# Other places for seven products, PReLU halves issued by engine, and a scaling done a unit ahead

## The chip, the cores and the metric

The kernel runs on one core of a Trainium2 chip. What counts is the device time of one execution in microseconds (us), as the median of several runs. A profile is one such execution, recorded by the hardware profiler.

The engines are named as the profile names them: PE is TensorE (PEld its weight loads), DVE is VectorE, ACT is ScalarE, POOL is GpSimd, SP is SyncE, which issues most DMAs. Each engine works through its own instructions in the order in which they were written.

## The reference, cut to what matters

A state-space block (4 sequences of 768 positions, 8 heads of 32, state of 16) feeds a feed-forward layer with a PReLU (3072 tokens, 256 wide, 2048 hidden).

```
for c in range(nc):                      # chunks of the sequence
    L = exp(cum[i] - cum[j]) * causal    # decay inside the chunk
    y = ((C @ B.T) * L) @ x + (C @ state) * exp(cum)
    state = exp(sum(la)) * state + (B * decay_from_j).T @ x
h = y @ w_in
g = np.maximum(h, 0.0) + alpha * np.minimum(h, 0.0)
out = g @ w_out
```

## The kernel before

**Work.** The tokens are cut into 6 groups of 512. Group 0 goes through the feed-forward layer as it stands, while weights are loaded (the first 102.6 us). Groups 1 to 5 use a scheme with seven instead of eight block products for each of the two matrix products: sums of weights (`ws`) and of tokens (`xs`) are formed beforehand, and seven products are combined into the four output blocks.

**Units.** A group g has four units, z = 0 to 3, each for 512 of the 2048 hidden features. A unit is the function `quad`. Its seven first products (`first`, two matmuls each) go into two PSUM banks, A and Y. ACT and DVE form the four hidden blocks g12, g22, g21 and g11 from them, each by a call of `prelu`; g12, g21 and g11 are read from a bank, g22 from `c22` in SBUF. Between g12 and g22 ACT copies `m1` into Y (L645), since Y is used again. POOL then forms four differences of the blocks (`ta`, `tb`, `tc_`, `td`, L650 and L659). The seven products with `w_out` of a unit (`product`, L592) are run within the next unit, at places that the table `places` gives.

**PReLU.** For each half p of a block, ACT multiplies by alpha (L600) and DVE takes the maximum (L601). In a PSUM bank both engines read the same bank, and the framework makes each wait until the other has left it.

**Order.** All engines' orders are written out by hand: `quad` calls `after(1)` to `after(14)` between its steps, and `after(j)` runs what the tables put there. `places` maps j to one of the products 1 to 7. `steps` maps (z, j) to a stage of the state-space work for the next group, which comes as two pairs of chunks, each in nine stages: transposes of B and C with `cd` (0), two stages that write `cz` and each run one scan for the decays `dec` (1, 2; L375, DVE), the state update from `bn` (3; L445 on PE), two scans for the second chunk (4, 5), two stages of Gram matmuls into the two buffers `ss`, each followed by two DVE products with `dec` (6, 7; L476, L481), and the output y with its copy to `xT` (8). A scan stands on DVE in the same queue as the PReLUs. `bn`, B scaled by decays, is formed on POOL in stage 0 (`pair_loads`, L327).

**Combine.** The seven products of a finished group lie in four PSUM banks. `combine` (L677 to L692) adds them up during z=0 of the next group, in steps at j = 5, 9, 13 and 14; one sum, `u4`, is formed on POOL and read by DVE (L692). `finish` transposes the two results on DVE (L703) and writes them out, at (1, 4) and (1, 5).

**Loads.** `load_pair` issues a pair's loads on SP: `nat` (B and C), `xt`, `ap` and the broadcast decays `abc`, a pair or two ahead.

Of the kernel before, what the change touches and what calls it, by code (L numbers as in the profile page):

```python
# [22 lines left out]
def kernel(  # L23
# [25 lines left out]
    nc = tc.nc  # L49
# [304 lines left out]
    def pair(gp):  # L354
# [27 lines left out]
        if gp == 0:  # L382
            ahead[0] = spread(z, 0)
            rows_turn(0, rows_scan(0))
        elif gp == 6:
            rows_turn(1, held["pr"])
        bn = pair_loads(gp)

        pf = ap
        if not abc:  # L390
# [204 lines left out]

    def prelu(o, h, z, i):

        for p in range(2):
            f = 4 * z + 2 * p + i
            nc.scalar.mul(o[:, p], h[:, p], s_alpha[:, f : f + 1])  # L600
            nc.vector.scalar_tensor_tensor(out=o[:, p], in0=h[:, p], scalar=s_mul[:, f : f + 1],  # L601
                                           in1=o[:, p], op0=ALU.mult, op1=ALU.max)

    def quad(g, z, after):


# [24 lines left out]
        first(A, lambda q: s2[:, q], t2)
        u2 = tile_of(wtp, "u2", "wg")
        nc.scalar.copy(out=u2, in_=A)  # L633
        after(4)
        after(5)
        nc.vector.tensor_tensor(out=Y, in0=Y, in1=u2, op=ALU.add)
        after(6)
        first(A, lambda q: wi[:, q, 1, 0], t3)
        c22 = tile_of(wtp, "c22", "wg")
        nc.vector.tensor_tensor(out=c22, in0=A, in1=m5, op=ALU.add)  # L640
        after(7)
        first(Y, lambda q: s4[:, q], b22)
        g12, g22, g21, g11 = (tile_of(gp, "gt", "gt") for i in range(4))
        prelu(g12, Y, z, 0)
        nc.scalar.copy(out=Y, in_=m1)  # L645
        prelu(g22, c22, z, 1)
        after(8)
        after(9)
        ta, tb, tc_, td = (tile_of(gp, "gt", "gt") for i in range(4))
        nc.gpsimd.tensor_tensor(out=tc_, in0=g22, in1=g12, op=ALU.subtract)  # L650
        after(10)
        first(A, lambda q: wi[:, q, 1, 1], t4)
        prelu(g21, A, z, 1)
        after(11)
# [12 lines left out]
    def combine(g):  # L667


        m = {n: ms[g][i][:, h] for n, (i, h) in HALVES.items()}  # L670
        sa = wtp.tile([P, 2, HT], F32, name="sa", tag="wr")
        u = wtp.tile([P, 2, HT], F32, name="u", tag="wr")
        u4 = op.tile([P, HT], F32, name="u4", tag="o_sb")
        c = [one.tile([P, 2, HT], F32, name=f"c{i}") for i in range(2)]
        last = g == NG - 1
        engs = [nc.sync, nc.scalar]
        nc.scalar.copy(out=sa[:, 0], in_=m[1])  # L677
        nc.vector.tensor_tensor(out=c[0][:, 0], in0=m[2], in1=sa[:, 0], op=ALU.add)
        if last:
            turn(g, 0, c[0], slice(0, HT), engs)  # L680
        yield
        nc.scalar.copy(out=sa[:, 1], in_=m[5])
        yield
        nc.vector.tensor_tensor(out=u[:, 0], in0=m[6], in1=sa[:, 0], op=ALU.add)
        nc.vector.tensor_tensor(out=u[:, 1], in0=m[7], in1=u[:, 0], op=ALU.add)
        nc.gpsimd.tensor_tensor(out=u4, in0=u[:, 0], in1=sa[:, 1], op=ALU.add)
        nc.gpsimd.tensor_tensor(out=c[1][:, 1], in0=u[:, 1], in1=sa[:, 1], op=ALU.add)
        yield
        nc.vector.tensor_tensor(out=c[1][:, 0], in0=u[:, 1], in1=m[4], op=ALU.subtract)
        if last:  # L690
            turn(g, 1, c[1], slice(0, GT), engs)
        nc.vector.tensor_tensor(out=c[0][:, 1], in0=m[3], in1=u4, op=ALU.add)  # L692
        ms.pop(g)
        if last:
            turn(g, 0, c[0], slice(HT, GT), engs)
        else:
            ends_of[g] = c

    def turn(g, i, c, ts, engs):
# [11 lines left out]
    def finish(g, i):  # L711
        turn(g, i, ends_of[g][i], slice(0, GT), [nc.sync])
# [28 lines left out]
    for n in range(2):  # L741
        for f in range(NF):
# [17 lines left out]
            if n and f in in_steps:  # L760
# [9 lines left out]

    places = {3: 1, 5: 2, 6: 3, 9: 5, 10: 7, 13: 6, 14: 4}
    for i in range(NZ * (NG - 1)):
        g, z = divmod(NZ + i, NZ)
        nxt = 2 * g + 2
# [1 line left out]
        def after(j, g=g, z=z, i=i, nxt=nxt):  # L776
            if i and j in places:
                product(*divmod(NZ + i - 1, NZ), places[j])
            if i == 0:
                if j in (3, 5, 6, 9):  # L780
                    output(NF - LAG + (j > 5), {3: 0, 5: 1, 6: 0, 9: 1}[j])
                if j == 2:
                    weight_sums(wi, in_sums, 4, 3)
                if j in (3, 5, 7):
                    weight_sums(wqt, out_sums, 0, {3: 0, 5: 1, 7: 2}[j])
                if j == 10:
                    weight_sums(wqt, out_sums, 0, 3)
            if i == 1 and j in (1, 4, 7, 9):
                weight_sums(wqt, out_sums, 4, {1: 0, 4: 1, 7: 2, 9: 3}[j])
            if g > 1 and z == 0 and j in (5, 9, 13, 14):  # L790
                if j == 5:
                    comb[0] = combine(g - 1)
                next(comb[0], None)
            if g > 1 and z == 1 and j in (4, 5):
                finish(g - 1, j - 4)
            if nxt < NP and (z, j) in steps:
                ssm(nxt + steps[z, j])
            if nxt < NP and (z, j) == (3, 6):
                token_sums(g + 1)
# [45 lines left out]
```

## Time and profile before

| | us |
|---|---|
| median of 3 runs | 471.69 (470.42 to 472.87) |
| the profiled execution's own time | 472.52 |
| its span, first to last instruction | 470.4 |
| mean granted PE clock, share of full speed | 0.954 |
| busy time of PE, DVE, POOL, ACT | 406.8, 269.5, 217.6, 183.8 |

A profile gives each engine's busy time and, for each idle stretch, the instruction whose end released the engine. The time of a run is a little longer than the span. Busy time on PE is modelled from overlapping matmuls; a row "x4" stands for the four records of two matmuls, and the start of the next row minus its own start is what they cost PE. PEclk is the clock that the chip granted to PE as a share of 2.4 GHz; 0.5 is 1.2 GHz.

### The profile page before, as it was taken

The page shows a single profiled execution, that of the slowest core. Times are in us where ns is not written, and L with a number is a line of the kernel's source. Part 1 is how long each engine was busy: PE and PEld are TensorE (multiplying, and loading weights), DVE is VectorE, ACT ScalarE, POOL GpSimd, SP SyncE. Part 2 cuts the span into 40 slices and gives each one's busy share as a digit, 9 for nine tenths or more (in the row PEclk, how much of TensorE's full clock was granted, in tenths as well). Part 3 has the DMA queues.
Part 4 walks back from the last instruction along what each step waited for, and adds up shares of the span by engine and source line. Part 5 has one row for each costly group of instructions (what it writes and reads, how often), then busy time and mean ns, then how long its engine had stood idle before and what let it go on. Part 6 is the DMA issues. An engine that isn't in the chain of part 4 may idle for free.

```text
span 470.4 us, 5917 instructions
## 1 busy us (share of the span) xinstructions
PE 406.8 (86%) x2131; PEld 302.9 (64%) x2131; DVE 269.5 (57%) x460; ACT 183.8 (39%) x408; POOL 217.6 (46%) x189
## 2 busy tenths in 40 slices
PE   6778899996998978599897869998859989989994
PEld 4446477785677667377585647766637767767773
DVE  5898966746457363548545555746363854353443
ACT  4556525235163263225433405326221543434430
POOL 2336745874835461607435232646260643453322
PEclk9999799999799998979998989999897999999998
DMA  9949961008506101055401017510102000002002
GB/s 215 258 157 247 220 138 49 1 8 191 100 2 111 36 1 45 0 81 125 86 0 46 1 23 125 100 46 0 46 0 45 1 1 1 0 5 42 0 0 46
DMA packets 124125, 30.58 MB, mean 65 GB/s; under 512 B 96880, under 2 KB 120000, under 8 KB 124096
## 3 DMA queue, kind: packets, MB, share of 16 engines
q1 hardware_dynamic: 117792, 29.67, 28.2%
q10 hardware_dynamic: 6304, 0.52, 0.9%
q8 instruction: 17, 0.28, 0.2%
q14 instruction: 12, 0.10, 0.1%
HBM read 26.85 MB, written 3.34 MB: 64 GB/s over the span
## 4 chain that ended last, share of the span: by engine, by line
PE 49%; DVE 22%; ACT 13%; POOL 10%; issue 4%; DMA 1%; POOLq 0%; ACTq 0%; DVEq 0%
PE hp L616 15%; PE bank L592 13%; DVE gt L601 12%; ACT gt L600 9%; POOL gt L659 7%; PE bank L535 5%; PE ss L476 4%; PE hp L522 4%; ACT hp L645 2%; DVE dec L375 2%; DVE dec L481 2%; PE ss L499 2%; DVE dec L370 1%; POOL xs L575 1%; PE ss L445 1%
## 5 line engine op out<-in xcount | busy, mean ns | idle before, releaser
L659 POOL TENSOR_TENSOR gt<-gt 128x512 f32<-128x512 f32 x58 | 91.2, 1572 | 36.1 <-DVE gt L601 25.4
L650 POOL TENSOR_TENSOR gt<-gt 128x512 f32<-128x512 f32 x20 | 32.1, 1603 | 136.4 <-DVE gt L601 121.7
L600 ACT ACTIVATE gt<-hp,s_alpha 128x256 f32<-128x256 f32 x120 | 54.5, 472 | 91.8 <-DVE gt L601 41.7
L592 PE MATMUL bank<-gt,w_out 128*128 128x256 f32 x320 | 87.1, 397 | 0.6 <-DVE gt L601 0.6
L601 DVE SCALAR_TENSOR_TENSOR gt<-hp,s_mul,gt 128x256 f32<-128x256 f32 x120 | 55.9, 480 | 48.3 <-ACT gt L600 48.2
L592 PEld LDWEIGHTS bank<-gt,w_out 128*128 128x128 f32 x320 | 62.6, 198 | 11.8 <-issue 1.5
L592 PE MATMUL bank<-gt,ws 128*128 128x256 f32 x240 | 63.8, 390 | 1.5 <-DVE c L692 1.5
L616 PE MATMUL hp<-xT,w_in 128*128 128x256 f32 x160 | 45.7, 409 | 15.4 <-DVE gt L601 11.2
L592 PEld LDWEIGHTS bank<-gt,ws 128*128 128x128 f32 x240 | 47.7, 199 | 9.1 <-DVE c L692 1.9
L375 DVE TENSOR_TENSOR_SCAN dec<-abc,ident_h 128x512 f32<-128x512 f32 x32 | 50.3, 1593 | 0.0
L616 PE MATMUL hp<-xs,ws 128*128 128x256 f32 x160 | 47.3, 421 | 2.4 <-DVE gt L601 2.4
L616 PEld LDWEIGHTS hp<-xT,w_in 128*128 128x128 f32 x160 | 27.7, 192 | 31.8 <-DVE gt L601 18.4
L616 PEld LDWEIGHTS hp<-xs,ws 128*128 128x128 f32 x160 | 30.1, 203 | 24.0 <-issue 10.5
L616 PE MATMUL hp<-xs,w_in 128*128 128x256 f32 x160 | 42.5, 389 | 0.0
L476 PE MATMUL ss<-cz,bh 64*128 64x512 f32 x80 | 28.2, 722 | 13.5 <-DVE dec L481 11.8
L481 DVE TENSOR_TENSOR dec<-ss,dec 128x512 f32<-128x512 f32 x40 | 25.8, 685 | 18.4 <-PE ss L476 18.4
L640 DVE TENSOR_TENSOR c<-hp,m 128x512 f32<-128x512 f32 x20 | 13.8, 692 | 35.2 <-PE hp L616 33.5
L616 PEld LDWEIGHTS hp<-xs,w_in 128*128 128x128 f32 x160 | 30.0, 193 | 5.4 <-issue 1.6
L633 ACT COPY u<-hp 128x512 f32<-128x512 f32 x20 | 11.8, 592 | 49.4 <-PE hp L616 49.4
L522 PE MATMUL hp<-xT,w_in 128*128 128x256 f32 x96 | 27.6, 412 | 3.8 <-DVE gt L526 3.8
L535 PE MATMUL bank<-w_out,gt 128*128 128x256 f32 x128 | 30.8, 383 | 0.0
L601 DVE SCALAR_TENSOR_TENSOR gt<-c,s_mul,gt 128x256 f32<-128x256 f32 x40 | 17.7, 483 | 21.9 <-ACT gt L600 21.9
(119 smaller groups left out, 538.8 us busy)
## 6 DMA issues: line engine op xcount, KB each, us to landing
abc<-z SPq DMA_DIRECT2D x20, 512.0 KB
raw<-in_moe_w_in_dram SPq DMA_DIRECT2D x8, 512.0 KB
raw<-in_moe_w_out_dram SPq DMA_DIRECT2D x8, 512.0 KB
xt<-in_x_dram SPq DMA_DIRECT2D x24, 128.0 KB
out_dram<-o_sb SPq DMA_DIRECT2D x34, 64.0 KB
nat<-in_B_dram SPq DMA_DIRECT2D x22, 64.0 KB
nat<-in_C_dram SPq DMA_DIRECT2D x22, 64.0 KB
ap<-pf SPq DMA_DIRECT2D x10, 128.0 KB
```

The lines of the kernel that those rows point to most:

```text
L375: nc.vector.tensor_tensor_scan(out=dv[:, k, ws], data0=abc[k][:, ws], data1=ident_h[:, ws], initial=0.0, op0=ALU.mult, op1=ALU.add)
L476: nc.tensor.matmul(gram[r].rearrange("p h t -> p (h t)"), bh[rs, k], cz[rs, :, k], start=True, stop=True, tile_position=(64 * r, 0), skip_ ...
L481: nc.vector.tensor_tensor(out=dec[:, k, hs], in0=gram[r], in1=dec[:, k, hs], op=ALU.mult)
L522: nc.tensor.matmul(hp, w_in[:, k, f * P : (f + 1) * P], xts[g][:, k, t0 : t0 + nt], start=(k == 0), stop=(k == KC - 1))
L535: nc.tensor.matmul(pos[0][t // 2][:, t % 2], gt[:, t * Q : (t + 1) * Q], w_out[:, f], start=(f == 0 and t % 2 == 0), stop=(f == NF - 1), s ...
L592: nc.tensor.matmul(ms[g][i][:, h], w, blocks[g, z][n][:, p], start=(q == 0 and h == 0), stop=(q == NQ - 1), skip_group_check=True)
L600: nc.scalar.mul(o[:, p], h[:, p], s_alpha[:, f : f + 1])
L601: nc.vector.scalar_tensor_tensor(out=o[:, p], in0=h[:, p], scalar=s_mul[:, f : f + 1], in1=o[:, p], op0=ALU.mult, op1=ALU.max)
L616: nc.tensor.matmul(to[:, p], w(2 * z + p), b, start=start and p == 0, stop=True, skip_group_check=True)
L640: nc.vector.tensor_tensor(out=c22, in0=A, in1=m5, op=ALU.add)
L650: nc.gpsimd.tensor_tensor(out=tc_, in0=g22, in1=g12, op=ALU.subtract)
L659: eng.tensor_tensor(out=o, in0=x0, in1=x1, op=ALU.subtract)
```

## The change

It has five parts. The products of a unit get other places, and two steps of `quad` move with them. `prelu` issues both ACT halves and then both DVE halves. `bn` is formed a unit ahead, at (1, 3) and (3, 8). `combine` no longer has `u4`: DVE adds the product with `u[:, 0]` first, and POOL adds `sa[:, 1]` to the result in place, as its last steps; `finish` moves to (1, 10) and (1, 13). The stages of the state-space work get other places.

```
-        elif gp == 6:
-            rows_turn(1, held["pr"])
-        bn = pair_loads(gp)
+        bn = bns.pop(gp) if gp in bns else pair_loads(gp)
...
     def prelu(o, h, z, i):
 
+        fs = [slice(4 * z + 2 * p + i, 4 * z + 2 * p + i + 1) for p in range(2)]
         for p in range(2):
-            f = 4 * z + 2 * p + i
-            nc.scalar.mul(o[:, p], h[:, p], s_alpha[:, f : f + 1])
-            nc.vector.scalar_tensor_tensor(out=o[:, p], in0=h[:, p], scalar=s_mul[:, f : f + 1],
+            nc.scalar.mul(o[:, p], h[:, p], s_alpha[:, fs[p]])
+        for p in range(2):
+            nc.vector.scalar_tensor_tensor(out=o[:, p], in0=h[:, p], scalar=s_mul[:, fs[p]],
                                            in1=o[:, p], op0=ALU.mult, op1=ALU.max)
...
         after(4)
+        nc.vector.tensor_tensor(out=Y, in0=Y, in1=u2, op=ALU.add)
         after(5)
-        nc.vector.tensor_tensor(out=Y, in0=Y, in1=u2, op=ALU.add)
-        after(6)
         first(A, lambda q: wi[:, q, 1, 0], t3)
         c22 = tile_of(wtp, "c22", "wg")
         nc.vector.tensor_tensor(out=c22, in0=A, in1=m5, op=ALU.add)
-        after(7)
+        after(6)
         first(Y, lambda q: s4[:, q], b22)
...
         prelu(g22, c22, z, 1)
+        after(7)
         after(8)
         after(9)
...
-        after(10)
         first(A, lambda q: wi[:, q, 1, 1], t4)
         prelu(g21, A, z, 1)
+        after(10)
         after(11)
...
-        nc.gpsimd.tensor_tensor(out=u4, in0=u[:, 0], in1=sa[:, 1], op=ALU.add)
-        nc.gpsimd.tensor_tensor(out=c[1][:, 1], in0=u[:, 1], in1=sa[:, 1], op=ALU.add)
+        if last:
+            nc.vector.tensor_tensor(out=u[:, 0], in0=u[:, 0], in1=sa[:, 1], op=ALU.add)
+            nc.gpsimd.tensor_tensor(out=c[1][:, 1], in0=u[:, 1], in1=sa[:, 1], op=ALU.add)
         yield
...
-        nc.vector.tensor_tensor(out=c[0][:, 1], in0=m[3], in1=u4, op=ALU.add)
+        nc.vector.tensor_tensor(out=c[0][:, 1], in0=m[3], in1=u[:, 0], op=ALU.add)
...
         else:
+            nc.gpsimd.tensor_tensor(out=c[0][:, 1], in0=c[0][:, 1], in1=sa[:, 1], op=ALU.add)
+            nc.gpsimd.tensor_tensor(out=c[1][:, 1], in0=u[:, 1], in1=sa[:, 1], op=ALU.add)
             ends_of[g] = c
...
-    places = {3: 1, 5: 2, 6: 3, 9: 5, 10: 7, 13: 6, 14: 4}
+    places = {3: 1, 5: 2, 8: 3, 9: 5, 11: 7, 13: 6, 14: 4}
...
-            if g > 1 and z == 1 and j in (4, 5):
-                finish(g - 1, j - 4)
+            if g > 1 and z == 1 and j in (10, 13):
+                finish(g - 1, j // 13)
...
-            if nxt < NP and (z, j) == (3, 6):
+            if nxt < NP and (z, j) == (3, 7):
                 token_sums(g + 1)
+            ahead = nxt + {(1, 3): 1, (3, 8): 2}.get((z, j), NP)
+            if ahead < NP:
+                if ahead == 6:
+                    rows_turn(1, held["pr"])
+                bns[ahead] = pair_loads(ahead)
```

How this moves instructions is shown at three places. The first is PE's order within a plain unit of the last group, before. `hp` is bank A or Y, `bank` holds the products' sums, and each row is a pair of matmuls; the first row reads the token sum `t2` and the last but one is the matmul that needs ACT's copy into Y.

```order
L616 MATMUL hp<-xs,ws_798 128x256 x2
L592 MATMUL bank<-gt,w_out 128x256 x2
L592 MATMUL bank<-gt,ws_1032 128x256 x2
L616 MATMUL hp<-xs,w_in 128x256 x2
L616 MATMUL hp<-xT,ws_799 128x256 x2
L592 MATMUL bank<-gt,ws_1030 128x256 x2
L592 MATMUL bank<-gt,w_out 128x256 x2
L616 MATMUL hp<-xs,w_in 128x256 x2
L616 MATMUL hp<-xT,w_in 128x256 x2
L592 MATMUL bank<-gt,ws_1031 128x256 x2
```

The same rows of the change:

```order
L616 MATMUL hp<-xs,ws_798 128x256 x2
L591 MATMUL bank<-gt,w_out 128x256 x2
L616 MATMUL hp<-xs,w_in 128x256 x2
L616 MATMUL hp<-xT,ws_799 128x256 x2
L591 MATMUL bank<-gt,ws_1032 128x256 x2
L591 MATMUL bank<-gt,ws_1030 128x256 x2
L616 MATMUL hp<-xs,w_in 128x256 x2
L591 MATMUL bank<-gt,w_out 128x256 x2
L616 MATMUL hp<-xT,w_in 128x256 x2
L591 MATMUL bank<-gt,ws_1031 128x256 x2
```

The product with `ws_1032` moved behind Y's last matmul (`ws_799`), and one product with `w_out` now stands between the matmul that reads `t4` and the one into Y after the copy.

The second place is ACT in a unit z=1, from g12's PReLU to g11's, with the semaphores that each instruction waits for, named after the engine that sets them (`c_...` is `c22`). Before:

```order
L600 ACTIVATE gt<-hp,s_alpha 128x256 [waits DVE_49,PE_49,Pool_49]
L600 ACTIVATE gt<-hp,s_alpha 128x256 [waits DVE_49]
L645 COPY hp<-m_1575 128x512 [waits DVE_49]
L600 ACTIVATE gt<-c_1645,s_alpha 128x256 x2
L409 COPY bh<-ss 128x256 [waits PE_49]
L600 ACTIVATE gt<-hp,s_alpha 128x256 [waits PE_49,Pool_49]
L600 ACTIVATE gt<-hp,s_alpha 128x256 [waits DVE_49]
L600 ACTIVATE gt<-hp,s_alpha 128x256 [waits PE_49,Activation_49]
L600 ACTIVATE gt<-hp,s_alpha 128x256 [waits DVE_49]
```

With the change:

```order
L599 ACTIVATE gt<-hp,s_alpha 128x256 [waits DVE_49,PE_49,Pool_49]
L599 ACTIVATE gt<-hp,s_alpha 128x256
L644 COPY hp<-m_1573 128x512 [waits DVE_49,Activation_49]
L599 ACTIVATE gt<-c_1609,s_alpha 128x256 x2
L505 COPY xT<-ss 128x256 [waits PE_49] x2
L599 ACTIVATE gt<-hp,s_alpha 128x256 [waits PE_49,Pool_49]
L599 ACTIVATE gt<-hp,s_alpha 128x256
L599 ACTIVATE gt<-hp,s_alpha 128x256 [waits PE_49,Activation_49]
L599 ACTIVATE gt<-hp,s_alpha 128x256
```

The second half of each PReLU out of a bank lost its wait for DVE; on DVE, the first half now waits for ACT and the second for nothing.

The third place is DVE at the end of z=0 and the start of z=1, from the combine on (rows `dec<-abc` are the scans, `dec<-ss,dec` the products with the Gram matmuls' results, `o_sb` the transposes of outputs). Before:

```order
L684 TENSOR_TENSOR u<-bank,sa 128x256
L685 TENSOR_TENSOR u<-bank,u 128x256
L375 SCALAR_TENSOR_TENSOR dec<-abc,ident_h 128x512
L689 TENSOR_TENSOR c_1974<-u,bank 128x256
L692 TENSOR_TENSOR c_1973<-bank,u_1972 128x256
L481 TENSOR_TENSOR dec<-ss,dec 128x512 x4
L703 STREAM_TRANSPOSE o_sb<-c_1973 128x512
L703 STREAM_TRANSPOSE o_sb<-c_1974 128x512
L636 TENSOR_TENSOR hp<-hp,u_2066 128x512
```

With the change:

```order
L683 TENSOR_TENSOR u<-bank,sa 128x256
L684 TENSOR_TENSOR u<-bank,u 128x256
L689 TENSOR_TENSOR c_1966<-u,bank 128x256
L692 TENSOR_TENSOR c_1965<-bank,u 128x256
L376 SCALAR_TENSOR_TENSOR dec<-abc,ident_h 128x512 x2
L480 TENSOR_TENSOR dec<-ss,dec 128x512 x2
L635 TENSOR_TENSOR hp<-hp,u_2060 128x512
L480 TENSOR_TENSOR dec<-ss,dec 128x512 x2
```

Both scans of the second chunk now stand together behind the four additions, `c_1965` reads no result of POOL, and the transposes have gone to later places among the PReLUs.

## Rows read from the trace of the kernel before

**Rows 1.** The page, part 1, TensorE: busy time, share of span, instructions.

```profile
PE 406.8 (86%) x2131; PEld 302.9 (64%) x2131; DVE 269.5 (57%) x460; ACT 183.8 (39%) x408; POOL 217.6 (46%) x189
```

**Rows 2.** Windows of groups 1 to 5: us, PE PEld DVE ACT POOL busy, PEclk, DMA.

```profile
102.60:169.87 67.27, 61.55 (x329) 45.21 (x327) 38.08 (x65) 28.20 (x63) 35.35 (x28) 0.95 0.39 78
169.87:247.32 77.45, 66.95 (x343) 49.75 (x342) 41.79 (x69) 28.76 (x66) 33.49 (x26) 0.93 0.26 51
247.32:323.29 75.97, 65.47 (x337) 48.44 (x336) 42.05 (x68) 28.52 (x65) 33.29 (x26) 0.96 0.27 53
323.29:401.06 77.77, 67.26 (x342) 49.64 (x341) 42.33 (x69) 28.35 (x64) 33.21 (x26) 0.93 0.06 14
401.06:457.26 56.20, 51.92 (x225) 41.31 (x224) 23.55 (x48) 23.91 (x51) 21.67 (x18) 1.00 0.06 10
```

**Rows 3.** Windows of group 3's units, a plain unit, group 1's first.

```profile
247.32:267.49 20.17, 15.56 (x66) 12.18 (x65) 10.74 (x17) 8.09 (x19) 8.57 (x6) 0.92 0.10 27
267.49:291.16 23.67, 19.49 (x108) 13.68 (x109) 12.31 (x23) 6.73 (x15) 7.31 (x7) 0.93 0.37 59
291.16:306.41 15.25, 13.73 (x65) 10.64 (x65) 11.44 (x16) 7.24 (x17) 9.51 (x6) 1.00 0.52 101
306.41:323.29 16.88, 16.69 (x100) 11.94 (x100) 7.57 (x15) 6.46 (x14) 7.89 (x8) 1.00 0.10 31
430.28:443.58 13.30, 12.82 (x58) 10.39 (x57) 5.00 (x11) 5.81 (x12) 5.08 (x4) 1.00 0.00 0
...
102.60:117.53 14.93, 11.16 (x58) 8.82 (x56) 10.04 (x20) 7.94 (x18) 6.33 (x6) 0.96 0.73 157
```

**Rows 4.** Timeline, last group: start us, us, engine line op out<-in, idle.

```profile
434.40 1.03 PE L592 MATMUL bank<-gt,w_out 128*128 128x256 f32 x4
...
434.60 0.59 ACT L633 COPY u<-hp 128x512 f32<-128x512 f32 x1 [1.14 <-PE hp L616]
...
435.26 1.03 PE L592 MATMUL bank<-gt,ws 128*128 128x256 f32 x4
...
438.10 0.47 ACT L600 ACTIVATE gt<-hp,s_alpha 128x256 f32<-128x256 f32 x1 [2.92 <-PE hp L616]
...
438.61 0.48 DVE L601 SCALAR_TENSOR_TENSOR gt<-hp,s_mul,gt 128x256 f32<-128x256 f32 x1 [0.73 <-ACT gt L600]
...
439.13 0.48 ACT L600 ACTIVATE gt<-hp,s_alpha 128x256 f32<-128x256 f32 x1 [0.55 <-DVE gt L601]
...
440.15 0.59 ACT L645 COPY hp<-m 128x512 f32<-128x512 f32 x1 [0.55 <-DVE gt L601]
...
440.68 0.90 ACT L600 ACTIVATE gt<-c,s_alpha 128x256 f32<-128x256 f32 x2
...
440.80 1.13 PE L616 MATMUL hp<-xT,w_in 128*128 128x256 f32 x4 [0.19 <-ACT hp L645]
...
441.22 0.88 DVE L601 SCALAR_TENSOR_TENSOR gt<-c,s_mul,gt 128x256 f32<-128x256 f32 x2 [1.10 <-ACT gt L600]
...
444.46 0.48 DVE L601 SCALAR_TENSOR_TENSOR gt<-hp,s_mul,gt 128x256 f32<-128x256 f32 x1 [0.54 <-ACT gt L600]
...
445.00 1.13 PE L616 MATMUL hp<-xs,ws 128*128 128x256 f32 x4 [0.29 <-DVE gt L601]
```

**Rows 5.** Timeline, group 3, z=0: two scans, PE's wait for `bn`.

```profile
249.72 3.61 DVE L375 TENSOR_TENSOR_SCAN dec<-abc,ident_h 128x512 f32<-128x512 f32 x2
...
255.04 0.44 PE L445 MATMUL ss<-xt,bn 128*64 128x128 f32 x4 [3.38 <-POOL bn L327]
```

**Rows 6.** Timeline, group 3, z=1: DVE's wait for `u4`, PE's for DVE.

```profile
274.45 0.42 DVE L692 TENSOR_TENSOR c<-bank,u 128x256 f32<-128x256 f32 x1 [2.80 <-POOL u L686]
...
274.79 1.28 DVE L481 TENSOR_TENSOR dec<-ss,dec 128x512 f32<-128x512 f32 x2
...
275.53 2.21 PE L476 MATMUL ss<-cz,bh 64*128 64x512 f32 x4 [3.93 <-DVE dec L481]
```

**Rows 7.** Line L375, DVE's scans: ns min/median/max, first and last start.

```profile
L375 DVE TENSOR_TENSOR_SCAN dec<-abc,ident_h x32: 1200/1386/2235, 104.9 to 381.3; 128x512 f32<-128x512 f32 x32
```

More of the change, by code (lines that the diff above doesn't have):

```diff
@@ L279 @@
     held = {}
+    bns = {}
     def rows_scan(i):
@@ L672, in combine @@
         u = wtp.tile([P, 2, HT], F32, name="u", tag="wr")
-        u4 = op.tile([P, HT], F32, name="u4", tag="o_sb")
         c = [one.tile([P, 2, HT], F32, name=f"c{i}") for i in range(2)]
@@ L764 @@
     token_sums(1)
-    steps = {(0, 1): 0, (0, 2): 0, (0, 3): 0, (0, 4): 0, (0, 10): 0, (0, 13): 0,
[3 rows of a table removed]
-    places = {3: 1, 5: 2, 6: 3, 9: 5, 10: 7, 13: 6, 14: 4}
+    steps = {(0, 1): 0, (0, 2): 0, (0, 3): 0, (0, 9): 0, (0, 14): 0,
[3 rows of a table added]
+    places = {3: 1, 5: 2, 8: 3, 9: 5, 11: 7, 13: 6, 14: 4}
     for i in range(NZ * (NG - 1)):
@@ L779, in after @@
             if i == 0:
-                if j in (3, 5, 6, 9):
-                    output(NF - LAG + (j > 5), {3: 0, 5: 1, 6: 0, 9: 1}[j])
+                if j in (3, 5, 8, 9):
+                    output(NF - LAG + (j > 5), {3: 0, 5: 1, 8: 0, 9: 1}[j])
                 if j == 2:
```

6 rows, old and new, of the table steps are left out of this document.

## The prediction

> **What bounds the kernel now.** I read the busy shares first: TensorE (PE) is busy 86% of the span [rows 1]. So the span is PE's work plus the places where PE stands still or runs at half speed. The windows by group of units find these places: from 102.60 us on, the kernel runs twenty units, and groups 2 to 4 take 76 to 78 us each at a mean clock of 0.93 to 0.96, while the last group, without state-space work, takes 56.20 at 1.00 [rows 2]. By unit, the two slow ones are z=0 (20.17 us) and z=1 (23.67), against 15.25, 16.88 and a plain 13.30 [rows 3].
>
> In the plain unit PE's fourteen pairs of matmuls follow each other every 0.865 us (434.40 to 435.26), so 14 x 0.865 = 12.1 us would do; 13.30 are taken [rows 3, 4]. The missing 1.2 us are waits, two of which the timeline rows show: the matmul at 440.80 waits for ScalarE's copy into Y, and the next unit's second matmul, at 445.00, for the DVE half of the last PReLU that starts at 444.46 [rows 4]. The PReLU chain is serial: ACT half (438.10), DVE half (438.61), ACT half (439.13), DVE half, and only then the copy at 440.15, 2.05 us after it began.
>
> In z=0, PE waits 3.38 us for GpSimd's `bn`, which stands behind three subtractions that the DVE scans beside them stretch [rows 5]. In z=1, PE waits 3.93 us for the DVE product with `dec`, because DVE itself waited 2.80 us for GpSimd's `u4`, again behind subtractions [rows 6]. After each such wait the granted clock sinks: those units show 0.92 and 0.93, the other two 1.00 [rows 3].
>
> **The change, part by part.** PReLU by engine: after it, ACT's second half has no wait on DVE, and DVE's first half waits for both ACT halves. Two ACT halves back to back take 0.90, two DVE halves 0.88 [rows 4]; with one hand-over of 0.02 the chain is 1.80 instead of 2.05, and the copy into Y starts 0.25 earlier. More is won behind it: ACT no longer stands while DVE works, so the third PReLU runs straight after the second, and the fourth ends about 2.9 us after its matmul starts instead of 4.1 (440.80 to 444.94). The Trainium skill ("PSUM — Partial Sum Buffer", PSUM bank collisions raise a hardware error) has it that two engines on one bank must be kept apart by semaphores. The trace agrees: the halves alternate, 438.10, 438.61, 439.13. By that rule no order of the halves would bring the chain of one PReLU under 1.80.
>
> Places of the products, in a plain unit: two pairs stand between Y's last matmul and the one that reads `t4`, as before, and a third now stands behind that, before the matmul that needs the copy into Y. This one starts five pairs instead of four (4.3 us) after Y's last matmul, whose copy is done 1.1 (matmul and its end) + 1.8 + 0.6 = 3.5 after it: no wait. The next unit's first two matmuls start eight and nine pairs after it, at 6.9 and 7.8. By then the PReLUs that they overwrite are done: the third's ACT halves end at 3.5 + 2 x 0.9 = 5.3, behind the second's, and its DVE halves 0.9 later, at 6.2; the fourth's at 4.3 + 2.9 = 7.2. No wait. The price: one pair instead of two covers ScalarE's copy `u2` (434.60, 0.59), so the matmul that needs it is released at 435.23 against a weight load due at 435.05, about 0.1 per unit. New unit: 12.2 us.
>
> `bn` a unit ahead: its instruction stays, off PE's path; the 3.38 go, and the state update stands after two more products. The early place needs `nat` a unit earlier; the loads are issued more than a unit before, so I cost it at nothing (if they were late, GpSimd and through it the products would wait). What is next in z=0: DVE's two scans (3.61 from 249.72, that is from 2.4 to 6.0 after the unit's start [rows 5]) stand before Y += u2 (0.7, an estimate by the products with `dec`, two in 1.28 [rows 6]), so Y's last matmul can start at 6.7 against 6.1: 0.6 lost, and 0.2 for `u2` behind the copies `cz`. Unit z=0: 12.1 + 0.6 (transposes) + 0.6 (state update) + 0.2 (weight loads laid open) + 0.8 = 14.3. The two 0.6 are estimates, bounded by z=2, whose PE is busy 13.73 against 12.82 in the plain unit [rows 3].
>
> `u4` gone: `c0` no longer waits for GpSimd, the 2.80 go. But both scans of the second half now stand behind the combine's four additions and before the first product with `dec`. From z=1's start: last PReLU 0.35, four additions of 0.42 make 2.0, two scans end at 5.6 at 1.8 each [rows 5], products with `dec` at 6.3 and 6.9. PE wants the two buffers at 5.6: 0.8 lost, not 3.93. The scan's cost is bounded by its shortest and longest, 1.20 and 2.24 [rows 7]: waits of 0 to 1.8. I take 1.8 us a scan, since GpSimd's subtractions lie beside. Unit z=1: z=3's work without its 0.5 of PReLU waits (16.4), 0.5 for transposes, 0.8: 17.7. Unit z=2: 12.1 + 0.6 + 0.2, and 0.2 since one scan stands before the third PReLU: 13.1. Unit z=3: 16.4.
>
> The Trainium skill ("SBUF — State Buffer", Who interferes with whom) speaks against this part: a VectorE instruction with two SBUF inputs and a GpSimd instruction that reads SBUF block each other whole. The trace agrees in kind: scans span 1.20 to 2.24 us [rows 7]. By that rule each of the two scans could sit out a whole subtraction, which is rival (a).
>
> Half clock: the units with PE's waits of 3 to 4 us have it, z=2, z=3 and the whole last group, with their waits of about 1 us, have not [rows 2, 3]. With no wait left above 0.8 in groups 2 to 4, I let it vanish there.
>
> Additions last and in place: the two GpSimd additions stay; one DVE addition and the `u4` buffer's wait change only the end, where matmuls hide them. The transposes of outputs, moved between the PReLUs of z=1, wait for these additions, done some 7 us into the unit; the first transpose is reached at 15.7.
>
> The sum of spans: groups 2 to 4, 14.3 + 17.7 + 13.1 + 16.4 = 61.5 each, instead of 77.45, 75.97, 77.77: -46.7. Last group: 4 x 12.2 + 0.3 = 49.1 instead of 56.20: -7.1. Group 1: z=0 has no products and keeps a wait of some 2 us before z=1, 13.1 instead of 14.93; z=1 between 17 without and 20 with half clock, 18.0; z=2 13.1; z=3 17.4, since the transposed rows now wait about 1 us for a buffer between its products. That is 61.6 instead of 67.27: -5.7. Together -59.5. The first 102.6 us and the end keep their order. 470.4 - 59.5 = 410.9 of span, plus the 2.1 around the profiled execution (472.52): 413.0. The three runs' median lies 0.8 below that execution; I leave the number at **413**.
>
> **Rivals.** (a) The scans set z=1: waits of 1.8, and half clock after them (some 3.4 us of PE work lost per group), 3 x (1.0 + 3.4) = 13 more: 426. For it: the scans do reach 2.24; against: the median of all is 1.39 [rows 7]. (b) The half clock stays though the waits shrink. The mean clocks price it: 0.05 x 67 + 0.07 x 77 + 0.04 x 76 + 0.07 x 78 = 17 [rows 2]: 430. Against: 1.00 in the units with waits of 1 us. (c) The PReLU edit gives only the hand-overs and the waits on it stay, 20 units x 1.1 = 22: 435. (d) Slower: DVE's transposes in z=1 wait for GpSimd's additions, hold up the fourth PReLU, and with it the next unit. GpSimd has 8 us to spare there; from then on each us costs one per group, and to eat 59 us over four groups it would have to come 23 us late in a unit of 18, while it is busy 7.31 [rows 3]. (e) Nothing comes of it, since another chain I missed paces groups 2 to 4: 470; against it speaks that no engine but PE is busy over 43 us of the 76 [rows 2].
>
> **How the numbers follow.** Within 0.5% is what a measurement of this kernel can hardly tell from no change (the runs spread by that). Forecast 0.56, its own range 403 to 421; (a) 0.14, (b) 0.13, (c) 0.09, all faster; an unforeseen loss of half the gain 0.03; (e) 0.02; (d) 0.03. So faster 0.95, same 0.02, slower 0.03. The low end is PE's work with no wait left: 9 to 10 us under the forecast. The high end takes in (a) and (b) and stops short of (c): 403 to 432.
>
> **What would show it.** Right: plain units 12.2 us apart, no PE wait on `bn` or `dec` over 1 us, clock 1.00 in groups 2 to 4, ACT's second half starting with no DVE wait. Wrong: PE waiting on `dec` in z=1 for over 2 us, clocks of 0.93 there, or DVE's transposes waiting for GpSimd. The likeliest error is a DVE wait in z=0 or z=1 that my order of events misses.

## The result, and the profile after

The changed kernel takes 416.11 us (median of 4 runs, 415.18 to 416.69), the kernel before, in the same comparison, 471.88: a ratio of 0.8818, 95% interval 0.879 to 0.8847. The forecast was 413, range 403 to 432.

The profile page of the changed kernel (its span is 414.5 us), part 1 and the clock line of part 2. The answer to [rows 1]: PE is busy 93% instead of 86%, with 23 us less busy time for as many matmuls. At most some 15 us of that come from fewer matmuls at half clock (the mean granted clock rose from 0.954 to 0.983, and 0.046 x 470 - 0.017 x 414 = 14.6). The rest is not the clock: a plain unit's busy time fell too, from 12.82 [rows 3] to 12.16, at 1.00 in both. In the clock line each digit is a fortieth of the span, 10.4 us; but for the last one, the low digits lie in the first six, ahead of the units.

```profile
PE 383.4 (93%) x2131; PEld 297.4 (72%) x2131; DVE 274.4 (66%) x461; ACT 179.7 (43%) x408; POOL 215.8 (52%) x188
...
PEclk9899969999999999999999999999999999999997
```

The windows of groups 1 to 5 of the changed kernel (stretch, its length, PE busy, granted clock, DMA). Against [rows 2], groups 2 to 4 fall from 76 to 78 us to 62 to 63, the last from 56.20 to 48.72, and every clock is 1.00, that is 2.4 GHz.

```profile
103.15:165.52 62.37, 58.26 (x330) 1.00 0.41 85
165.52:228.27 62.75, 60.68 (x342) 1.00 0.32 63
228.27:291.09 62.82, 60.46 (x338) 1.00 0.32 64
291.09:353.23 62.14, 60.68 (x342) 1.00 0.08 18
353.23:401.95 48.72, 48.72 (x225) 1.00 0.07 11
```

By unit, answering to [rows 3]: group 1's first, the four of group 3, a plain one. In the last three PE is busy for the whole of the window. In z=0 and z=1 it still stands for 1.2 us each.

```profile
103.15:117.38 14.23, 11.12 (x57) 1.00 0.59 118
228.27:243.06 14.79, 13.60 (x66) 1.00 0.12 37
243.06:261.77 18.71, 17.54 (x109) 1.00 0.02 4
261.77:274.73 12.96, 12.96 (x67) 1.00 0.82 153
274.73:291.09 16.36, 16.36 (x102) 1.00 0.45 85
365.46:377.62 12.16, 12.16 (x57) 1.00 0.01 1
```

What PE still waits for from 95 us on (us in total, times, longest). The waits on `bn` are gone, those on `dec` are three of 1.2 instead of three of up to 3.93 [rows 6].

```profile
PE ss L475 <- DVE dec L480: 3.5, 3, 1.2
PE hp L616 <- DVE hp L635: 2.0, 3, 1.1
PE hp L616 <- DVE gt L601: 1.7, 1, 1.7
PE hp L616 <- ACT u L633: 1.4, 1, 1.4
PE ss L311 <- ACT xT L505: 1.0, 1, 1.0
```

The timeline of the changed kernel at three places. First group 3's z=0, answering to [rows 5]: two scans start beside GpSimd's three subtractions and take 4.27 us, Y += u2 comes behind them, and PE's matmul into Y waits 1.07. Then z=1, answering to [rows 6]: `u4` is gone, but the two scans, again beside three subtractions, take 4.42, and the products with `dec` behind them free the first buffer for the second pair of Gram matmuls 1.17 late, the second later still (that row costs 1.65, up to 251.61, instead of 1.06). Last a plain unit, answering to [rows 4]: ACT's two halves, DVE's two halves, the copy into Y 1.89 after the start, and the matmul into Y at 375.03 with no wait.

```profile
229.00 4.76 POOL L659 TENSOR_TENSOR gt<-gt 128x512 f32<-128x512 f32 x3
...
230.57 4.27 DVE L376 TENSOR_TENSOR_SCAN dec<-abc,ident_h 128x512 f32<-128x512 f32 x2
...
235.48 1.13 PE L616 MATMUL hp<-xT,ws 128*128 128x256 f32 x4 [1.07 <-DVE hp L635]
...
244.91 4.42 DVE L376 TENSOR_TENSOR_SCAN dec<-abc,ident_h 128x512 f32<-128x512 f32 x2
...
249.96 1.72 PE L475 MATMUL ss<-cz,bh 64*128 64x512 f32 x4 [1.17 <-DVE dec L480]
...
371.83 0.84 ACT L599 ACTIVATE gt<-hp,s_alpha 128x256 f32<-128x256 f32 x2 [2.13 <-PE hp L616]
372.76 0.88 DVE L601 SCALAR_TENSOR_TENSOR gt<-hp,s_mul,gt 128x256 f32<-128x256 f32 x2 [1.15 <-ACT gt L599]
373.72 0.59 ACT L644 COPY hp<-m 128x512 f32<-128x512 f32 x1 [1.05 <-DVE gt L601]
375.03 1.03 PE L616 MATMUL hp<-xT,w_in 128*128 128x256 f32 x4
```

### The profile page after: what moved, and what is told of

The parts are those of the page before. It is cut to its first block, busy times and chain, and to the rows that moved or that the text cites. A ratio compares the mean times of both kernels' runs of the same rounds, so it can differ in the third digit from the quotient of the medians.

```text
span 414.5 us, 5967 instructions
## 1 busy us (share of the span) xinstructions
PE 383.4 (93%) x2131; PEld 297.4 (72%) x2131; DVE 274.4 (66%) x461; ACT 179.7 (43%) x408; POOL 215.8 (52%) x188
## 4 chain that ended last, share of the span: by engine, by line
PE 73%; DVE 18%; ACT 5%; issue 1%; POOL 1%; DMA 1%; DVEq 0%; ACTq 0%; POOLq 0%
PE hp L616 26%; PE bank L591 25%; DVE dec L376 6%; PE bank L534 5%; PE ss L475 5%; PE hp L521 4%; PE ss L498 2%; DVE dec L371 2%; ACT gt L599 2%; DVE dec L480 1%; DVE wr L227 1%; DVE gt L601 1%; DVE gt L525 1%; PE ss L491 1%; PE ss L444 1%
## 5 line engine op out<-in xcount | busy, mean ns | idle before, releaser
L659 POOL TENSOR_TENSOR gt<-gt 128x512 f32<-128x512 f32 x58 | 90.6, 1563 | 25.3 <-DVE gt L601 11.6
L591 PE MATMUL bank<-gt,w_out 128*128 128x256 f32 x320 | 82.1, 380 | 0.0
L601 DVE SCALAR_TENSOR_TENSOR gt<-hp,s_mul,gt 128x256 f32<-128x256 f32 x120 | 51.9, 478 | 45.3 <-ACT gt L599 41.4
L599 ACT ACTIVATE gt<-hp,s_alpha 128x256 f32<-128x256 f32 x120 | 49.9, 469 | 71.5 <-PE hp L616 70.3
L650 POOL TENSOR_TENSOR gt<-gt 128x512 f32<-128x512 f32 x20 | 28.7, 1437 | 62.0 <-DVE gt L601 55.7
L591 PE MATMUL bank<-gt,ws 128*128 128x256 f32 x240 | 58.9, 381 | 0.0
L376 DVE TENSOR_TENSOR_SCAN dec<-abc,ident_h 128x512 f32<-128x512 f32 x32 | 55.3, 1759 | 0.0
L616 PE MATMUL hp<-xT,w_in 128*128 128x256 f32 x160 | 41.4, 381 | 1.7 <-DVE gt L601 1.7
L616 PE MATMUL hp<-xs,ws 128*128 128x256 f32 x160 | 42.3, 387 | 0.0
L616 PEld LDWEIGHTS hp<-xs,w_in 128*128 128x128 f32 x160 | 28.1, 189 | 13.1 <-issue 7.4
L521 PE MATMUL hp<-xT,w_in 128*128 128x256 f32 x96 | 27.6, 412 | 3.8 <-DVE gt L525 3.8
L534 PEld LDWEIGHTS bank<-w_out,gt 128*128 128x128 f32 x128 | 24.7, 193 | 3.5
L459 POOL TENSOR_TENSOR sm<-state,bmask 128x256 f32<-128x256 f32 (+1 forms) x12 | 7.7, 638 | 37.2 <-DVE state L455 37.2
```

The costliest lines, as they stand in the source:

```text
L376: nc.vector.tensor_tensor_scan(out=dv[:, k, ws], data0=abc[k][:, ws], data1=ident_h[:, ws], initial=0.0, op0=ALU.mult, op1=ALU.add)
L521: nc.tensor.matmul(hp, w_in[:, k, f * P : (f + 1) * P], xts[g][:, k, t0 : t0 + nt], start=(k == 0), stop=(k == KC - 1))
L534: nc.tensor.matmul(pos[0][t // 2][:, t % 2], gt[:, t * Q : (t + 1) * Q], w_out[:, f], start=(f == 0 and t % 2 == 0), stop=(f == NF - 1), s ...
L591: nc.tensor.matmul(ms[g][i][:, h], w, blocks[g, z][n][:, p], start=(q == 0 and h == 0), stop=(q == NQ - 1), skip_group_check=True)
L599: nc.scalar.mul(o[:, p], h[:, p], s_alpha[:, fs[p]])
```

## The experiments

The theory under test is that of the prediction: the gain is three waits (the PReLU chain, `bn`, `u4`) and the half clock behind the longer two. The rivals are that one of them gives little, or that something else removes it. All times are medians, ratios are against the kernel before in the same comparison.

| kernel | us | ratio, 95% interval |
|---|---|---|
| before + PReLU by engine | 449.88 | 0.9523, 0.949 to 0.9557 |
| before + `bn` ahead | 456.01 | 0.9649, 0.9622 to 0.9676 |
| before + no `u4` | 460.49 | 0.9721, 0.9664 to 0.9778 |
| changed, PReLU undone | 425.61 | 0.9021, 0.8989 to 0.9054 |
| changed, `u4` back | 431.11 | 0.912, 0.9078 to 0.9162 |
| changed, `bn` undone | 437.03 | 0.9251, 0.922 to 0.9282 |
| the same, late state update | 415.62 | 0.8804, 0.8769 to 0.884 |
| changed, without differences | 407.62 | 0.8634, 0.8619 to 0.865 |
| changed, scan behind Gram | 409.33 | 0.8673, 0.866 to 0.8686 |
| changed, scan behind Y += u2 | 411.62 | 0.8722, 0.8707 to 0.8736 |
| both scan moves | 405.15 | 0.8595, 0.8569 to 0.8621 |
| changed, made to wait | 435.52 | 0.9214, 0.9185 to 0.9244 |

**The PReLU part alone, and all but it.** The edit of `prelu` shown above, made to the kernel before.

> The kernel before with the PReLU halves issued by engine and nothing else. Theory (the halves as such free the chain): the two waits that the plain unit shows, 0.19 on the copy into Y and 0.29 on the last DVE half, go, and up to 1.1 per unit; 20 units x 0.7 = 14 us, to about 458 (455 to 462), the last group to 53 to 54.5 us. Rival (c) (only the hand-overs go): 467 to 471. Rival (the whole 1.1 per unit comes from the halves, none from the places): 450, the last group at 49 to 51. GpSimd's `bn` and `u4` waits of 3 to 4 us and the half clock behind them stay by every theory.

449.88: the second rival, that the halves give the whole of it; the last group, 51.81, is 0.8 longer than this rival allowed, since z=1 there still waits 1.44 for `u4`. PE's waits from 102 us on, first of the kernel before, then of this one; the copy into Y goes from 16 waits to 2, DVE's PReLU halves from 21 to 8.

```profile
PE hp L616 <- DVE gt L601: 13.6, 21, 2.8
...
PE hp L616 <- ACT hp L645: 4.2, 16, 1.0
```

```profile
PE hp L617 <- DVE gt L602: 5.1, 8, 2.3
...
PE hp L617 <- ACT hp L646: 1.1, 2, 0.8
```

What let ACT run ahead shows in its own waits. In the kernel before, from 102 us on, ACT waits 60 times for a DVE half of a PReLU; with this edit there is no such row left.

```profile
ACT gt L600 <- DVE gt L601: 41.7, 60, 1.7
```

The last unit takes 12.29 (422.81 to 435.10), almost the 12.16 of the changed kernel, so the places of the products add 0.1 there. In the opposite direction, `prelu` interleaved again in the changed kernel:

```
...
         for p in range(2):
-            nc.scalar.mul(o[:, p], h[:, p], s_alpha[:, fs[p]])
-        for p in range(2):
...
+            f = 4 * z + 2 * p + i
+            nc.scalar.mul(o[:, p], h[:, p], s_alpha[:, f : f + 1])
...
```

> The changed kernel with the PReLU halves interleaved again (ACT, DVE, ACT, DVE). Theory: the copy into Y still comes in time (1.1 + 2.05 + 0.6 = 3.75 us against five pairs, 4.3), but the last PReLU of a unit ends 1.2 us later, at 8.4 against the next unit's second matmul at 7.8, so 0.6 us per unit, 20 units: 428 (424 to 432), the last group at 51 us. Rival 1 (the places alone do it): 416, the last group at 49. Rival 2 (the halves are the whole gain of the plain unit): 436 to 438, the last group at 53.

425.61, 0.47 per unit, inside the theory's range: units of the last group 12.23, 12.74 and 13.39 (starts 359.83, 372.06, 384.80, 398.19). So either the halves or the places remove most of the plain unit's waits: without the `u4` wait the last group takes 54.7 before, 50.4 with the halves alone, 50.9 with the places and no halves, and 48.7 with both. The two overlap, and 21.8 alone becomes 9.5 on top of the rest.

**`bn`.** Undone in the changed kernel, the places kept:

```
-        bn = bns.pop(gp) if gp in bns else pair_loads(gp)
+        elif gp == 6:
+            rows_turn(1, held["pr"])
+        bn = pair_loads(gp)
...
-            ahead = nxt + {(1, 3): 1, (3, 8): 2}.get((z, j), NP)
-            if ahead < NP:
-                ...
```

> The changed kernel with `bn` formed in stage 0 of its own unit again, so that the state update at (0, 9) has only its later place. Theory 1 (my step: forming `bn` ahead removes the 3.38 us wait): the wait comes back less the distance of two more products and a pair, 3.38 - 2.6 = 0.8 us, 3 or 4 times: 419. Theory 2 (the place alone removes it, since GpSimd's subtractions end 4.5 us ahead of the state update): 416, no wait on `bn`. Rival (the whole wait and the half clock come back): 430 or more.

437.03: the rival's time, but not its place. In z=0 there is no wait, as theory 2 says: the state update at (0, 9) comes late enough. The wait is in z=2. The change moved stage 0 of that pair from (1, 10) to (1, 14), that is on GpSimd's queue from ahead of the three subtractions of z=1 to behind them, and with `bn` back in stage 0 it stands there too, ahead of a state update at (2, 3). The timeline of this kernel in z=2 of group 3, and the windows of z=2 in groups 2, 3 and 4:

```profile
273.59 5.55 POOL L661 TENSOR_TENSOR gt<-gt 128x512 f32<-128x512 f32 x3 [2.81 <-PE ss L406]
279.11 0.63 POOL L328 TENSOR_TENSOR bn<-nat,prt 128x256 f32<-128x256 f32 x1
...
279.80 0.66 PE L446 MATMUL ss<-xt,bn 128*64 128x128 f32 x8 [3.43 <-POOL bn L328]
```

```profile
204.40:223.82 19.42, 15.99 (x67) 0.82 0.83 147
...
273.61:290.06 16.45, 13.02 (x66) 1.00 0.91 159
...
339.85:357.69 17.84, 14.41 (x62) 0.90 0.16 28
```

Does the place alone hide `bn` in z=2 too? Beside the edit above:

```
-             (1, 14): 1, (2, 1): 1, (2, 2): 1, (2, 3): 1, (2, 9): 1, (2, 14): 1,
+             (1, 14): 1, (2, 1): 1, (2, 2): 1, (2, 8): 1, (2, 9): 1, (2, 14): 1,
```

> The kernel with `bn` back in stage 0 of its own unit, which waited in z=2 and not in z=0, with the state update of z=2 moved from (2, 3) to (2, 8), about where z=0 has its own. Theory (a late place alone hides `bn`; forming it ahead is needed only where the update stands early): no wait on `bn` in groups 1 to 4, 416 (414 to 419), the time of the changed kernel. Rival (GpSimd's queue needs the early `bn` wherever the update stands): 425 or more.

415.62, with no wait on `bn` in the units: in z=2 too, a late state update is worth as much as an early `bn`. The other way round, the early `bn` alone in the kernel before (the edit of the change, nothing else):

> The kernel before with `bn` formed a unit ahead and nothing else. Theory: the 3.38 us wait of z=0 goes, and with it its share of the half clock, 3 x (3.4 - 0.6 + 2.7) = 16.5: 455 (451 to 459). Rival (the wait passes on to Y += u2, which stands behind two scans of 3.6 us): 3 x 2 = 6, 462 to 468, with PE waits on `hp` from VectorE of 2 us in z=0.

456.01, the theory. z=0 of group 3 takes 15.10 at clock 1.00 instead of 20.17 at 0.92 [rows 3].

```profile
241.65:256.75 15.10, 13.87 (x66) 1.00 0.12 36
```

**`u4`.** Back in the changed kernel:

```
-        if last:
-            nc.vector.tensor_tensor(out=u[:, 0], in0=u[:, 0], in1=sa[:, 1], op=ALU.add)
-            nc.gpsimd.tensor_tensor(out=c[1][:, 1], in0=u[:, 1], in1=sa[:, 1], op=ALU.add)
+        nc.gpsimd.tensor_tensor(out=u4, in0=u[:, 0], in1=sa[:, 1], op=ALU.add)
+        nc.gpsimd.tensor_tensor(out=c[1][:, 1], in0=u[:, 1], in1=sa[:, 1], op=ALU.add)
...
-        nc.vector.tensor_tensor(out=c[0][:, 1], in0=m[3], in1=u[:, 0], op=ALU.add)
+        nc.vector.tensor_tensor(out=c[0][:, 1], in0=m[3], in1=u4, op=ALU.add)
```

> The changed kernel with `u4` formed on GpSimd again, ahead of the sum on VectorE, and GpSimd's second addition back beside it. Theory (the wait of z=1 came from `u4`): in z=1 the two scans start 4 us later, behind GpSimd's subtractions, but run at 1.2 us each without them; the wait on `dec` in groups 2 to 4 grows from 1.17 to about 3.6, and the half clock comes back in three groups: 3 x (2.5 + 2.7) + 1 = 17, 433 (428 to 437). Rival 1 (one such wait brings no half clock): 424. Rival 2 (the later places of the scans hide `u4`): 416 to 418.

431.11, the theory. The timeline in group 3's z=1: DVE waits 3.50 for `u4`, the two scans then take 2.90 with GpSimd's subtractions over (`bn` alone lies beside them), PE waits 3.25, and its next rows run at half clock (1.86 us up to the next row where 0.97 are usual).

```profile
252.86 0.43 DVE L692 TENSOR_TENSOR c<-bank,u 128x256 f32<-128x256 f32 x1 [3.50 <-POOL u L686]
253.20 2.90 DVE L376 TENSOR_TENSOR_SCAN dec<-abc,ident_h 128x512 f32<-128x512 f32 x2
...
256.74 2.67 PE L475 MATMUL ss<-cz,bh 64*128 64x512 f32 x4 [3.25 <-DVE dec L480]
259.34 2.07 PE L616 MATMUL hp<-xs,w_in 128*128 128x256 f32 x4
```

In the kernel before, `u4` removed and the transposes of outputs moved (the same lines the other way, and `finish` at (1, 10) and (1, 13)):

> The kernel before without `u4`: VectorE adds u first, GpSimd adds in place at the end, and the transposes of outputs stand at (1, 10) and (1, 13). Theory: the wait of 3.93 us on `dec` goes in groups 2 to 4, with its half clock, and 1.5 in the last group: 3 x (3.9 + 2.7) + 1.5 = 21, 451 (446 to 455). Rival (the half clock stays on account of the `bn` wait): 458 to 460.

460.49, 9 short of the theory and next to the rival's time, but only in part for the rival's reason. Its four runs spread from 456.83 to 462.05, at mean clocks of 0.988 to 0.962. The windows of z=0, z=1, z=2 of group 2:

```profile
169.13:190.56 21.43, 16.83 (x70) 0.84 0.08 24
190.56:210.06 19.50, 17.62 (x104) 1.00 0.04 7
210.06:226.66 16.60, 13.94 (x64) 1.00 0.77 144
```

z=1 does get full clock and falls to 19.5 to 19.7 in groups 2 to 4. That is 4.0 to 5.4 less than before and not the 6.6 of the theory, since a wait of 1.0 on `dec` stays there. z=2 costs 1.35 more than in [rows 3]: PE waits there 0.29 for DVE's PReLU halves and 1.14 for Y += u2. The trace puts the second of these down to the transposes of outputs, which now stand among the PReLUs: one of them (211.34 to 212.04) lies between the last PReLU of z=1 and the scans of z=2, and Y += u2 starts 8.07 after the unit's start (218.13) where it was 6.72 in group 3 of the kernel before. No run separates the two. z=0 keeps its `bn` wait and half clock, which is the rival, and costs some 1.2 more than before in two groups of three.

**The waits that are left.** First, are the scans of z=0 and z=1 long because GpSimd works beside them?

```
+        cut = z in (0, NZ - 1) and g < NG - 1
...
-        for o, x0, x1 in ((ta, g12, g11), (tb, g22, ta), (td, tb, g21)):
+        for o, x0, x1 in () if cut else ((ta, g12, g11), (tb, g22, ta), (td, tb, g21)):
...
```

> The changed kernel without GpSimd's last three differences (`ta`, `tb`, `td`) in units z=0 and z=3 of groups 1 to 4; the products read g11, g21 and g22 in their place, so this part of the result is not computed. These are the differences that lie beside VectorE's scans in z=0 and z=1. Theory (they stretch the scans): the pairs of scans of 4.27 and 4.42 us become 2.4 to 2.9, the waits of z=0 on `hp` (1.07) and of z=1 on `dec` (1.17, and 0.6 more behind it) go, 3 us per group in groups 2 to 4, 1 in group 1: 406 (404 to 409). Rival (the scans take that long by themselves, or the waits have another source): 414 to 417, scans as long as before.

407.62, the theory, and PE's waits on `dec` and on `hp` from Y += u2 are gone. The timeline of DVE in group 3, z=0 and z=1: 2.33 and 2.81 for the two scans; the second pair still lies beside GpSimd's two additions.

```profile
227.50 2.33 DVE L376 TENSOR_TENSOR_SCAN dec<-abc,ident_h 128x512 f32<-128x512 f32 x2
...
240.50 2.81 DVE L376 TENSOR_TENSOR_SCAN dec<-abc,ident_h 128x512 f32<-128x512 f32 x2
```

Second, without leaving anything out: in z=1 the first Gram product goes between the two scans, which it does not need both of.

```
+        swap = fine and gp % 2 == 0
         if fine:
-            for w in range(2):
+            for w in range(1 if swap else 2):
                 half_decays(1, w)
                 yield
...
         for k in range(2):
+            if swap and k:
+                half_decays(1, 1)
+                yield
```

> The changed kernel with the first Gram product and its two products with `dec` ahead of the second of the two scans at the start of z=1. Theory (two scans at 2.2 us stand before the products that free the buffers; my term of 0.8 was really 1.8): the wait on `dec` goes in groups 2 to 4, 3 x 1.8 = 5.4: 410.7 (409 to 412). Rival (the second scan then holds up Y += u2 or the second products with `dec`, and the wait only moves): 414 to 417, with a new wait of PE on `hp` in z=1.

409.33: the theory, and 1.4 us better. In the profiled execution 1.0 of that lies ahead of the units (they start at 102.18 instead of 103.15), where nothing was changed, and 0.45 in z=1 of group 1. DVE's timeline in group 3's z=1: scan, products with `dec`, scan. PE has no wait on `dec` left in the units.

```profile
241.71 2.28 DVE L376 TENSOR_TENSOR_SCAN dec<-abc,ident_h 128x512 f32<-128x512 f32 x1
243.91 1.26 DVE L484 TENSOR_TENSOR dec<-ss,dec 128x512 f32<-128x512 f32 x2
245.09 1.73 DVE L376 TENSOR_TENSOR_SCAN dec<-abc,ident_h 128x512 f32<-128x512 f32 x1
```

Third, the second scan of z=0 behind Y += u2, and then both moves.

```
-    steps = {(0, 1): 0, (0, 2): 0, (0, 3): 0, (0, 9): 0, (0, 14): 0,
+    steps = {(0, 1): 0, (0, 2): 0, (0, 5): 0, (0, 9): 0, (0, 14): 0,
```

> The changed kernel with the second scan of z=0, and the two copies `cz` ahead of it, behind Y += u2 instead of before it. Theory (my term of 0.6 + 0.2 for z=0 is that scan and those copies): PE's wait on `hp` (0.16 to 1.07) and its 0.3 on `u2` go in z=0 of groups 2 to 4 and in part in group 1: 3 x 1.2 + 0.5, 412 (410.5 to 414). Rival (the scan then holds up `c22` and the PReLU behind it, which start 2 us later, and PE waits there): 415 to 418.

> Both edits together: the first Gram product ahead of the second scan in z=1, and the second scan of z=0 behind Y += u2. Theory (the two waits are independent): the sum of both, 416.1 - 5.4 - 4.1 = 406.6 (404.5 to 409), no wait of PE over 0.5 us in groups 2 to 4. Rival (scans moved into z=0's middle meet GpSimd less, and one of the edits alone already gives all there is): 410 to 412.

411.62 and 405.15: both as the theory has them, and the two are independent. 405.15 beats both kernels; against the changed one that is 2.5% (0.8595 / 0.8818 = 0.975). Its PE waits from 90 us on are three, all in group 1:

```profile
PE hp L620 <- DVE gt L605: 1.7, 1, 1.7
PE ss L311 <- ACT xT L509: 1.0, 1, 1.0
PE hp L620 <- ACT u L637: 0.7, 1, 0.7
```

Some 1.1 us of its gain in the profiled execution lie ahead of the units (they start at 102.01 instead of 103.15): the low clock of the sixth digit above is not there. Nothing was changed in that stretch.

**The clock.** Waits of known size in the last group, where no state-space work disturbs:

```
+        if g == NG - 1:
+            scr = op.tile([P, GT], F32, name="o_sb")
+            for _ in range(2 * z + 2):
+                nc.vector.tensor_tensor(out=scr, in0=m5..., in1=m5..., op=ALU.add)
         nc.vector.tensor_tensor(out=Y, in0=Y, in1=u2, op=ALU.add)
```

> The changed kernel with 2, 4, 6 and 8 extra additions on VectorE (m5 + m5 into a tile that nobody reads) ahead of Y += u2 in units z=0 to 3 of the last group, so that PE waits some 1.0, 2.4, 3.8 and 5.1 us there, in a stretch with no state-space work. Theory (my step: waits up to about 2 us leave the clock at full, waits of 3.4 and more bring it to half): 416.1 + 12.3 + 2 x 3.4 = 435 (431 to 438), granted clock 1.00 in z=0 and z=1, about 0.9 in z=2 and z=3. Rival 1 (half clock after every wait over 1 us): 1.00 nowhere, 440 or more. Rival 2 (a wait alone does not do it): 1.00 in all four, 428.

435.52. The time is the theory's, its parts are not quite: the waits were 0.45, 3.06, 3.42 and 4.87, since some additions lay beside GpSimd's subtractions and took up to 1.6 us instead of 0.7. That the time fits is partly luck: the waits add up to 11.8 instead of 12.3, and the clock fell in three units instead of two. The windows of the first three units, and the rows of the second from its wait on:

```profile
353.25:366.20 12.95, 12.50 (x58) 1.00 0.00 1
366.20:384.64 18.44, 15.38 (x57) 0.81 0.00 1
384.64:402.18 17.54, 14.12 (x58) 0.90 0.18 30
```

```profile
374.68 2.07 PE L616 MATMUL hp<-xT,ws 128*128 128x256 f32 x4 [3.06 <-DVE hp L640]
376.55 3.62 PE L591 MATMUL bank<-gt,ws 128*128 128x256 f32 x8
```

So a wait of 3 us in a plain unit is followed by rows at 1.2 GHz (eight records in 3.41 us, up to 379.96, instead of 1.73), and z=1 costs 6.3 more than 12.16 for a wait of 3.06. That refutes rival 2 and supports the step by which the half clock vanishes with the long waits. The other half of the theory, full clock behind waits of up to about 2 us, is not tested here: no wait came out between 0.45 and 3.06.

## Why the prediction was right

The forecast stood 3.1 below the median, and 3.6 below in the span (410.9 against 414.5). By its own terms:

- **Plain unit, 12.2:** 12.16. The chain ahead of the copy is 1.89 instead of 1.80, and the last PReLU ends 3.2 after its matmul starts (375.03 to 378.22) instead of 2.9, behind a transpose of outputs that stands ahead of it on DVE; in the next unit, without one, it is 2.87 (387.20 to 390.07). All are still hidden. The last group is 48.72 against 49.1. Rival (c) is refuted by the PReLU part alone, -21.8 us: ACT's 60 waits for DVE are gone with it, where by (c) 467 to 471 was due.
- **`bn`:** the 3.38 went, and the size was right (456.01 alone where 455 was expected). The mechanism was incomplete: in z=0 the later place of the state update suffices, and the early `bn` is needed for z=2, whose stage 0 I had not followed to its place behind GpSimd's subtractions. Undone, it costs 20.9 us.
- **`u4`:** the 2.80 went, as forecast; back in, it costs 15.0.
- **z=1, 17.7:** 18.49, 18.71 and 18.73. This is the term that was mis-sized: 0.8 lost was 1.8 (1.17 of wait and 0.6 in the row behind it). I took 1.8 us for a scan where 2.2 were due, two in 4.42. Rival (a) has the right wait, 1.8, and the wrong consequence: no half clock follows it. Taking GpSimd's subtractions away, or one scan, removes the wait.
- **z=0, 14.3:** 14.72, 14.79 and 14.09. The 0.8 were up to 1.37 (1.07, and 0.3 on `u2`), by the same long scans; moving one of them gives 4.5 us over the program.
- **z=2 and z=3, 13.1 and 16.4:** 12.74 to 12.96, and 16.36 to 16.58, in groups 2 to 4.
- **Group 1, 61.6:** 62.37. z=0 took 14.23, not 13.1: PE waits 1.39 for `u2`, behind ScalarE's copies, with fewer matmuls to cover it. The other three units missed by -0.6, -0.4 and +0.6, which cancel in part by luck. The 1.0 us wait of the transposed rows is there (1.0, on ACT's xT).
- **Half clock:** none in any unit; rival (b) is refuted. That clock and not waiting is a good part of the price is seen with `u4` back: PE's waits on `dec` grow by 6.2 in all (3.5 to 9.7), the time by 15.
- **Start and end:** the units start at 103.15 instead of 102.60, and the end takes 12.55 after them instead of 13.1. Neither was forecast, and that the two cancel is luck.

The differences are +3.2 in groups 2 to 4 (187.7 against 184.5), +0.8 in group 1, -0.4 in the last, and nothing for start and end: 3.6. Against the median it is 3.1, since an execution took 1.7 us beside its span and not the 2.1 that I had added.

Rivals (d) and (e) did not come up: the first transpose is reached at 259.88, 9 us after GpSimd's additions end (250.5).

**Alone and together.** The three parts alone give 21.8, 16.8 and 12.3, that is 50.9 of the 55.8; undone one at a time from the whole they cost 9.5, 20.9 and 15.0. These sums need not agree, since the parts share the half clock (undone, `u4` costs 15.0 of which 6.2 are waits) and the halves share their gain with the places. The other two parts of the change, the places of the products and of the state-space stages, were not run alone. That they supply the missing 4.9 us, by keeping a wait from moving to the next queue, is likely but not shown.

## What to carry to other kernels

Cost an instruction on VectorE by what GpSimd does at that moment, not by its median: here that was the difference between 1.2 and 2.2 us. Before an operation is formed earlier, ask whether its reader may simply stand later; undoing one part of a change at a time shows which of the two is at work. On PE, count a wait of 3 us as 5 to 6: the matmuls behind it mostly run at half clock.

## What the runs showed of the hardware

**Scans and subtractions take turns.** Two scans take 2.33 us beside an idle GpSimd, a subtraction 1.27 us beside an idle VectorE. In z=0 of group 3 the first of the three subtractions is over (230.26) before the scans begin. The second (230.34 to 231.61) keeps its 1.27, and the scan that starts at 230.57 takes 2.12. The third then starts beside the scan that is still running and takes 2.06, and the second scan (232.61 to 234.84) takes 2.22.

```profile
231.69 2.06 POOL L659 TENSOR_TENSOR gt<-gt 128x512 f32<-128x512 f32 x1
```

These two subtractions and two scans fill 230.34 to 234.84, 4.50 us, where the work of the one behind that of the other would be 2.33 + 2 x 1.27 = 4.87: nearly no overlap. The Trainium skill ("SBUF — State Buffer", Who interferes with whom) says that a VectorE instruction with two SBUF inputs contends with a GpSimd instruction that reads SBUF, and calls the port pair that they share an exclusive lock. The trace agrees within 8%, and by that rule z=1 would have been forecast better than by my 1.8: a scan that sits out a subtraction is 1.17 + 1.27 = 2.44, the measured one 2.21.

**The same wait, two clocks.** With `bn` undone, z=2 has a wait of 3.43 us in groups 2, 3 and 4; the granted clock of these units is 0.82, 1.00 and 0.90. In the same execution z=1 waits 1.18, 1.17 and 1.17 us for `dec`, and in group 2 alone the rows behind it run at half clock (192.77 to 194.46, 1.69 us, where 0.97 are usual). In the changed kernel itself the three waits of 1.2 us were followed by full clock. So the length of a wait does not settle by itself whether 1.2 GHz follows. Over all traces, in the units, rows at 1.2 GHz came within 2 us of the end of a wait in 31 of 32 waits of 2.31 to 4.87 us, and in one of 84 waits of 0.9 to 2.20 us. What sets it in the two odd cases stays open.
